# Channels dealt to partitions by threes, one set of convolution diagonals, and row casts on VectorE instead of casting DMAs

## The chip, the cores and the metric

One core of one Trainium2 chip. The metric is the device time of one execution in microseconds (us); the profile's span, from its first to its last instruction, is 1.6 to 2.0 us shorter than that in the runs quoted here. A ratio is the mean time of one kernel's fast runs over the mean of the fast runs of the kernel before in the same rounds, so it is not quite the ratio of the medians that stand beside it.

## The reference

A causal convolution over 7 tokens, with one softmax-normalised set of taps per head (8 heads of 24 channels), then a two-matrix network with the activation h / (1 + exp(-beta h)):

```python
w = softmax(weight, axis=-1)                       # weight: (8, 7)
out = einsum('hk,bskhg->bshg', w, x_unf)           # x: (8, 4096, 192), x_unf: 7 shifted tokens, zeros in front
x = out.reshape(32768, 192)
h = x @ w_in                                       # (192, 2048)
g = h * (1 / (1 + exp(-beta * h)))
y = g @ w_out                                      # (2048, 192), float32
```

## The kernel before

Tokens are worked on in 32 chunks of 1024 (512 from each half of the batch). The 192 channels are cut into three groups of 64; the two batch halves fill the 128 partitions. The matmuls are bf16.

Rows are brought in by casting DMAs on the POOL queue to a buffer in DRAM, then by one large transposing DMA:

```python
def cast(ch):                        # two casting DMAs per chunk, DRAM to DRAM
    ...
    for h in range(2):
        nc.gpsimd.dma_start(out=xd[r0:, :, h, :],
            in_=x_v[p, t0:t1, h, :].rearrange("t (c d) -> t c d", c=NG))
def xpose(ch):                       # one transposing DMA per chunk
    nc.sync.dma_start_transpose(new_xt(ch)[:, :, r0:], xd[r0:].rearrange("t c h d -> t (c h d)"))
```

From the third chunk on the convolution is done on VectorE. A partition's channel differs from group to group, so its taps do too, and a step covers one group (512 columns):

```python
scalar = cw[:, j, k : k + 1]
nc.vector.scalar_tensor_tensor(out=dst, in0=src, scalar=scalar, in1=dst, op0=ALU.mult, op1=ALU.add)
```

The first chunk's convolution runs on TensorE, as seven matmuls with a diagonal matrix for each group. Its start-up matters here:

```python
load_x(x0, 0)                        # SP queue: rows of the first chunk, 2 x 384 KB
load_x(x1, TOK)                      # rows of the second chunk, 2 x 384 KB
... w_out, 4 x 384 KB
load_w_in(0)                         # POOL queue: casting DMA, first quarter of w_in to 64 partitions
...
copy_w_in(0)                         # VectorE: the same weights to partitions 64 to 127
new_ct(0)
for c in range(NG):
    ...                              # 7 diagonal matmuls into pv
    if c < 2:
        nc.vector.tensor_scalar_mul(cts[0][:, c, :], pv, rn[:, c : c + 1])
    else:
        nc.scalar.mul(cts[0][:, c, :], pv, rn[:, c : c + 1])
    if c == 0:
        for b in range(NB):
            cast_rows(x1b, x1, b)    # VectorE casts the second chunk's rows
```

Each chunk then takes 16 steps of six hidden matmuls, one activation on ScalarE and sixteen output matmuls; an output accumulator is reduced on VectorE when it is full.

## Time and profile before

| | before |
|---|---|
| timed runs | 696.6 to 697.2 us, median 697.0 |
| the profiled run | 698.47 us, span 696.7 us |
| PE / ScalarE / VectorE / POOL busy | 99% / 83% / 76% / 9% |
| one chunk in mid-run | 20.9 us |

From the page of the kernel before: the busy time of each engine, and the chain of work that ended last, by engine and by line.

```profile
PE 688.6 (99%) x11339; PEld 497.9 (71%) x11339; DVE 528.2 (76%) x814; ACT 578.5 (83%) x532; POOL 60.6 (9%) x75
...
PE 98%; DMA 1%; ACT 0%; DVE 0%; issue 0%; ACTq 0%
```

The stage table of one chunk (stretch, its length, then busy us of PE, weight loads, VectorE, ScalarE and POOL with the number of instructions, the granted clock, the DMA share and GB/s):

```profile
58.57:79.50 20.93, 20.93 (x358) 15.24 (x356) 18.87 (x29) 17.84 (x17) 10.04 (x12) 1.00 2.08 167
```

PE is busy for all of the chunk, so VectorE and POOL can only matter where PE waits. These places are at the start. TensorE's timeline of the kernel before there (start, length, engine, line, operation; in brackets the idle time in front and what ended it):

```profile
8.82 0.26 PE L293 MATMUL pa<-ident,beta_q 16*128 16x16 f32 x1 [1.43 <-DMA beta_q<-in_moe_beta_dram]
...
9.05 4.97 PE L279 MATMUL ph<-xt,diag 128*128 128x512 f32 x14
13.86 1.79 PE L279 MATMUL pa<-xt,diag 128*128 128x512 f32 x7
15.58 1.47 PE L411 MATMUL ph<-ct,w_in_s 64*128 64x512 bf16 x12
```

In this execution the convolution (L279) starts at 9.05 us, held by the transpose of beta and its DMA, and the twelve first hidden matmuls (L411) run through from 15.58 us. VectorE at that time:

```profile
12.43 0.75 DVE L323 TENSOR_SCALAR ct<-ph,rn 128x512 bf16<-128x512 f32 x1 [0.46 <-PE ph L279]
13.09 1.15 DVE L230 CAST x1b<-x 128x384 bf16<-128x384 f32 x4
14.16 0.74 DVE L323 TENSOR_SCALAR ct<-ph,rn 128x512 bf16<-128x512 f32 x1
```

The casts of the second chunk's rows (x1b) stand between the two convolved columns that VectorE writes, but their data is there: no idle time in front of them.

VectorE's groups over ten chunks in mid-run (out<-in, shapes, count, busy us, mean ns of one, idle time in front):

```profile
L395 DVE SCALAR_TENSOR_TENSOR ct<-xt,cw,ct 128x512 bf16<-128x512 bf16 x181 | 123.2, 745 | 0.0
...
L393 DVE TENSOR_SCALAR ct<-xt,cw 128x512 bf16<-128x512 bf16 x30 | 9.5, 345 | 0.0
```

The chunk of the stage table is an early one, in which VectorE works ahead (24 of these steps, where a chunk has 21 of its own); in mid-run it is busy for 16.4 us of a chunk (164.45 us in ten).

### The profile page before, as it was taken

How to read it: one execution, taken by the hardware profiler on the slowest of the kernel's cores; microseconds unless marked ns; L12 is line 12 of the kernel's file. 1: busy time of each engine (PE TensorE's matmuls, PEld its weight loads, DVE VectorE, ACT ScalarE, POOL GpSimd, SP SyncE). 2: the span in 40 equal slices, each digit the busy share in tenths (PEclk: the TensorE clock that was granted, in tenths of full speed). 3: DMA queues.
4: the chain of work that ended last, by engine and by line, in shares of the span. 5: the costliest groups of instructions: out<-in, count | busy, mean ns of one | idle time of the engine just before them, and what ended most of it. 6: DMA issues, size and time to landing. Idle time of an engine off the chain costs nothing.

```text
span 696.7 us, 24650 instructions
## 1 busy us (share of the span) xinstructions
PE 688.6 (99%) x11339; PEld 497.9 (71%) x11339; DVE 528.2 (76%) x814; ACT 578.5 (83%) x532; POOL 60.6 (9%) x75
## 2 busy tenths in 40 slices
PE   8999999999999999999999999999999999999997
PEld 5477777777777777777777777777777777777776
DVE  4998888977787777787777787777787777787322
ACT  4888888888888888888888888888888888888883
POOL 3724554100000000000000000000000000000000
PEclk9999999999999999999999999999999999999999
DMA  8999999922211223211232211322221222211111
GB/s 226 102 151 168 172 172 176 159 61 71 59 48 49 70 59 71 59 44 53 70 59 71 60 44 50 72 58 70 60 44 52 70 60 71 59 36 37 47 36 59
DMA packets 183064, 54.95 MB, mean 79 GB/s; under 512 B 146336, under 2 KB 182960, under 8 KB 182960
## 3 DMA queue, kind: packets, MB, share of 16 engines
q0 software_dynamic: 96544, 12.92, 29.0%
q1 hardware_dynamic: 86368, 40.45, 24.8%
q8 instruction: 88, 1.44, 0.9%
q14 instruction: 16, 0.13, 0.1%
q10 hardware_dynamic: 48, 0.01, 0.0%
HBM read 28.98 MB, written 37.29 MB: 95 GB/s over the span
## 4 chain that ended last, share of the span: by engine, by line
PE 98%; DMA 1%; ACT 0%; DVE 0%; issue 0%; ACTq 0%
PE ph L411 47%; PE pa L441 25%; PE pb L441 24%; DMA beta_q<-in_moe_beta_dram 1%; PE ph L279 1%; PE pb L279 0%; PE pa L279 0%; ACT g L419 0%; ACT L159 0%; DVE xt L346 0%; DVE w_out_s L308 0%; PE pb L220 0%; ACTq L138 0%; PE ph L213 0%; PE pb L237 0%
## 5 line engine op out<-in xcount | busy, mean ns | idle before, releaser
L419 ACT ACTIVATE g<-ph,beta 128x1024 bf16<-128x1024 f32 x512 | 570.0, 1114 | 99.1 <-PE ph L411 95.0
L441 PEld LDWEIGHTS <-g 64*128 64x128 bf16 x8192 | 352.3, 94 | 121.2 <-issue 1.7
L411 PE MATMUL ph<-ct,w_in_s 64*128 64x512 bf16 x3072 | 415.1, 376 | 0.6 <-ACT g L419 0.6
L395 DVE SCALAR_TENSOR_TENSOR ct<-xt,cw,ct 128x512 bf16<-128x512 bf16 x552 | 375.9, 745 | 0.0
L441 PE MATMUL pa<-w_out_s,g 64*128 64x192 bf16 x4128 | 234.1, 243 | 0.4 <-ACT g L419 0.4
L441 PE MATMUL pb<-w_out_s,g 64*128 64x192 bf16 x4064 | 224.5, 243 | 0.0
L411 PEld LDWEIGHTS <-w_in_s 64*128 64x128 bf16 x3072 | 141.9, 94 | 62.0 <-issue 0.9
L460 DVE TENSOR_REDUCE osb<-pa 128x384 f32<-128x768 f32 x64 | 61.3, 958 | 121.9 <-PE pa L441 121.5
L460 DVE TENSOR_REDUCE osb<-pb 128x384 f32<-128x768 f32 x63 | 60.0, 953 | 31.2 <-PE pb L441 31.1
L104 POOL DMA_DIRECT2D xd<-in_x_dram x60 | 54.4, 909 | 49.7 <-DMA xd<-in_x_dram 48.4
L393 DVE TENSOR_SCALAR ct<-xt,cw 128x512 bf16<-128x512 bf16 x92 | 30.3, 359 | 0.2 <-DMA xt<-xd 0.2
L213 PE MATMUL ph<-zeros 128*128 128x512 bf16 (+2 forms) x13 | 5.3, 475 | 1.3 <-DVE warm L158 1.3
L325 ACT ACTIVATE ct<-pa,rn 128x512 bf16<-128x512 f32 x1 | 0.7, 687 | 5.8 <-PE pa L279 5.8
L457 ACT COPY osb<-pb 128x192 f32<-128x192 f32 x1 | 0.3, 319 | 5.8 <-PE pb L441 5.8
L279 PE MATMUL ph<-xt,diag 128*128 128x512 f32 x14 | 5.0, 520 | 0.0
L192 DVE COPY w_in_s<-w_in_s 64x1536 bf16<-64x1536 bf16 x4 | 3.0, 760 | 1.8 <-DMA w_in_s<-in_moe_w_in_dram 1.7
L279 PEld LDWEIGHTS ph<-xt,diag 128*128 128x128 f32 x14 | 3.6, 259 | 1.0
L346 DVE COPY xt<-pb 128x768 bf16<-128x768 bf16 x2 | 1.9, 958 | 2.6 <-PE pb L237 2.6
L308 DVE TENSOR_TENSOR w_out_s<-w_out_raw,beta_r 128x768 bf16<-128x768 f32 x4 | 3.8, 948 | 0.0
L279 PE MATMUL pb<-xt,diag 128*128 128x512 f32 x7 | 3.5, 497 | 0.0
L279 PEld LDWEIGHTS pb<-xt,diag 128*128 128x128 f32 x7 | 1.3, 186 | 3.0 <-issue 3.0
L213 PEld LDWEIGHTS <-zeros 128*128 128x128 bf16 x13 | 1.6, 129 | 2.2 <-DVE warm L158 1.3
(58 smaller groups left out, 37.5 us busy)
## 6 DMA issues: line engine op xcount, KB each, us to landing
out_dram<-osb SPq DMA_DIRECT2D x127, 192.0 KB, 2.1
xd<-in_x_dram POOLq DMA_DIRECT2D x54, 198.0 KB, 15.1
x<-in_x_dram SPq DMA_DIRECT2D x4, 384.0 KB, 4.6
w_out_raw<-in_moe_w_out_dram SPq DMA_DIRECT2D x4, 384.0 KB, 9.6
xd<-in_x_dram POOLq DMA_DIRECT2D x6, 192.0 KB, 15.4
w_in_s<-in_moe_w_in_dram POOLq DMA_DIRECT2D x4, 192.0 KB, 8.6
xt<-xd SPq DMA_TRANSPOSE x30, 4.6
out_dram<-osb SPq DMA_DIRECT2D x2, 96.0 KB, 1.8
```

The source lines that it names most:

```text
L104: nc.gpsimd.dma_start(out=xd[r0:, :, h, :], in_=x_v[p, t0:t1, h, :].rearrange("t (c d) -> t c d", c=NG),)
L192: nc.vector.tensor_copy(w_in_s[DG : 2 * DG, :, cols], w_in_s[0:DG, :, cols])
L213: nc.tensor.matmul(pf[:, 0, 0:cols], zeros[:, 0:128], zeros[:, 0:cols], start=True, stop=True)
L279: nc.tensor.matmul(pv, diag[:, c, k, :], xt[:, o : o + TOK], start=(k == 0), stop=(k == K - 1))
L308: nc.vector.tensor_tensor(w_out_s[:, fcs, :], w_out_raw[:, fcs, :], beta_r[:, fcs].unsqueeze(2).to_broadcast((128, NQ, D)), ALU.mult,)
L346: nc.vector.tensor_copy(xt[:, :, t : t + 2 * BLK].rearrange("p c (q b) -> p c q b", b=2), halves[i].rearrange("p c b q -> p c q b"),)
L393: nc.vector.tensor_scalar_mul(dst, src, scalar)
L395: nc.vector.scalar_tensor_tensor(out=dst, in0=src, scalar=scalar, in1=dst, op0=ALU.mult, op1=ALU.add)
L411: nc.tensor.matmul(ph[:, h, :], w_in_s[rows, j, fc * 128 : (fc + 1) * 128], cts[s][rows, j, :], start=(j == 0), stop=(j == NG - 1),)
L419: nc.scalar.activation(gs[s][:, fc], ph, AF.Silu, scale=beta[:, fc : fc + 1])
L441: nc.tensor.matmul(self.po[:, r, b * D : (b + 1) * D], g[rows, fc, self.h, q * BLK : (q + 1) * BLK], w_out_s[rows, fc, :], start=(self.don ...
L460: nc.vector.tensor_reduce(dst, self.po[:, :, 0 : nb * D].rearrange("p r n -> p n r"), axis=mybir.AxisListType.X, op=ALU.add,)
```

## The change

Channel 3p + c goes to partition p of group c. All three groups of a partition then belong to one head and share its taps: one set of seven diagonals in place of three, one spread matmul in place of three, and one VectorE step of 1536 columns in place of three of 512. Rows come in as fp32 by ordinary DMAs, VectorE casts them and deals out the channels, and four small DMAs per chunk transpose them from SBUF. Less prominent, the first quarter of w_in is now loaded as fp32, twice, ahead of the second chunk's rows, and cast on ScalarE; and the transpose of beta moves behind 14 convolution matmuls.

```diff
+    def load(ch): ...                # two fp32 DMAs per chunk, SP queue
+    def cast(ch, h):
+        nc.vector.tensor_copy(xbs[ch][:, :, :, h, :],
+            xfs[ch][:, h].rearrange("q b (p c) -> q b c p", c=NG))
     def xpose(ch):
-        nc.sync.dma_start_transpose(new_xt(ch)[:, :, r0:], xd[r0:]...)
+        for b in range(NB):
+            nc.sync.dma_start_transpose(xt[:, :, HALO + b * BLK : HALO + (b + 1) * BLK],
+                xbs[ch][:, b].rearrange("q c h p -> q (c h p)"))
 ...
     load_x(x0, 0)
+    for r in range(2):
+        nc.sync.dma_start(out=w_in_raw[r * DG : (r + 1) * DG], in_=w_in_v[:, :, 0:FW])
     load_x(x1, TOK)
 ...
-    load_w_in(0)
 ...
-    pb = pc[:, 1, 0:NF]
-    nc.tensor.transpose(pb, beta_q, ident[0:NF, 0:NF])
 ...
+    nc.scalar.copy(w_in_s[:, :, 0:FW], w_in_raw)
 ...
-    copy_w_in(0)
 ...
+        if c == 1:
+            pb = in_b()[:, 0, 0:NF]
+            nc.tensor.transpose(pb, beta_q, ident[0:NF, 0:NF])
+            nc.vector.tensor_copy(beta, pb)
+            nc.vector.reciprocal(beta_r, beta)
 ...
-            src = xts[s][:, j, o : o + TOK]
-            scalar = cw[:, j, k : k + 1]
+            src = xts[s][:, c0:, o : o + TOK]
+            scalar = cw[:, k : k + 1]
```

(The tap loop, the halo copies and the places where loads, casts and steps are queued change with it.)

## The prediction

> **What bounds the kernel now.** TensorE. The page gives PE 99% busy of a 696.7 us span, VectorE 76%, ScalarE 83%; the chain that ended last is 98% PE. In the stage table a chunk of 1024 tokens takes 20.92 us (37.65 to 58.57, 58.57 to 79.50), 1.307 us for each of 16 steps: six 512-column hidden matmuls in three pairs and eight pairs of 192-column output matmuls. These stream 3072 columns, 2.35 per ns: almost no gap is left. 32 chunks are 669 us. The other 28 are the start (first hidden matmul at 15.58 us), extra work and stalls in the first chunk, and the end.
>
> **The repeated part.** No repeated PE or ScalarE work changes. On VectorE, per chunk, 18 multiply-add steps of 512 columns (start to start 0.67 us in the timeline) and 3 first steps (0.27) become 6 steps of 1536 columns (my estimate 1.74 us: 1600 ns at one column per 0.96 GHz cycle, plus the 0.14 left over in 0.67) and one first step (0.54): 12.9 us becomes 11.0. Added are two row casts of 768 columns with source step 3 (estimate 0.55 to 1.0 us each, from the 384-column cast's 0.31) and the halo copy (0.16). With four reductions at 0.88 that is 16 to 17 us of 20.92, as before (16.4). VectorE stays off the critical path: a finished accumulator waits for at most 3 us of queued VectorE work, and its bank is needed again about 5 us later. POOL loses its 60 casting DMAs; nothing on the chain waits for them. The four small transposes per chunk are issued about 15 us before their first reader; one large one took about 5 us. I expect 20.9 us per chunk again.
>
> **What reaches the critical path: the start.**
> - The beta transpose waited for its DMA (6.05 us on the chain) and held the first convolution matmul until 9.05 us; it moves behind 14 of these. They then wait for the last copy of transposed rows (ends 7.83) and one set of diagonals; strided row casts may add 0.3 us each. First convolution matmul at 8.0 to 8.6 us: 0.5 to 1.1 gained.
> - Part of it is lost: these matmuls follow each other every 0.42 us until about 11.5 us, then every 0.22. The Trainium skill, "TensorE: Matmul & The Clock Gate", section "What's actually happening", states that the array runs at half clock until one busy window of about 3.4 us, and that the window is free-running; the two spacings agree. If the switch stays at its time, an earlier start runs more matmuls slowly.
> - The later weight spread takes 0.83 us of PE for six matmuls; two remain: about 0.5 us saved where PE stalls.
> - The end is unchanged.
>
> **Predicted:** 695.8 us (before 697.1), 80% range 694.0 to 697.6. Faster by over 2%: 1%; within 2%: 96%; slower by over 2%: 3%.
>
> **What would show each step.** Stage table: 20.9 us per chunk. Groups: 1536-column step near 1.8 us, cast under 1.1. VectorE share 70 to 78%, POOL under 2%. Timeline: first convolution matmul at 8.0 to 8.6 us, first hidden one at 14.5 to 15.2 (before 15.58). Waits: no mid-run PE wait on VectorE or DMA.
>
> **What would make it wrong.** Row casts or 1536-column steps so slow that VectorE passes 20.9 us per chunk; transposes so slow to issue on the SP queue that convolution starts late or output stores queue; VectorE blocked in the first chunk on the third chunk's transposes (its first step is queued before the first reduction); the first weights, now loaded as fp32 ahead of the second rows, arriving late.

## More of the kernel before

All runs used here are of state fast.

The profiled run is over 1 us slower than every timed run beside it.

## The result, and the profile after

The changed kernel took 698.05 us (median of 4 fast runs, 697.18 to 698.35) against 696.98 us; ratio 1.0014, 95% interval 0.9996 to 1.0031. It is the same within 2%, as forecast, but outside the stated range of 694.0 to 697.6. In three later controls, on chips 9, 0 and 9 again, it gave 1.0044, 1.0050 and 1.0020: there it is slower by 0.2 to 0.5%, clear of the intervals, and less steady than the kernel before.

| | before | after |
|---|---|---|
| median | 696.98 us | 698.05 us |
| span of the profile | 696.7 us (a late start) | 696.2 us |
| VectorE / POOL busy | 76% / 9% | 75% / 1% |
| one chunk in mid-run | 20.9 us | 20.9 us |

The two spans alone would say that the change won 0.5 us. They mislead, since the first profile fell on an execution that was late at its start (run b_again below).

From the page of the changed kernel, the engines and the chain:

```profile
PE 687.9 (99%) x11332; PEld 521.2 (75%) x11332; DVE 524.8 (75%) x472; ACT 577.9 (83%) x526; POOL 3.5 (1%) x13
...
PE 95%; DMA 2%; DVE 1%; SPq 1%; ACT 0%; issue 0%; DVEq 0%
```

The stage table of one chunk, and VectorE's groups over ten chunks in mid-run:

```profile
58.60:79.50 20.90, 20.90 (x357) 16.02 (x354) 16.45 (x15) 17.81 (x17) 0.00 (x0) 1.00 0.35 96
```

```profile
L395 DVE SCALAR_TENSOR_TENSOR ct<-xt,cw,ct 128x1536 bf16<-128x1536 bf16 x61 | 110.8, 1816 | 1.1
...
L106 DVE CAST xb<-xf 128x768 bf16<-128x768 f32 x20 | 13.6, 679 | 0.0
L393 DVE TENSOR_SCALAR ct<-xt,cw 128x1536 bf16<-128x1536 bf16 x10 | 10.0, 1003 | 0.0
```

The repeated part did what was forecast: the same 20.9 us, VectorE 16.45 us of it, PE without a gap. On VectorE the longer steps save 12.4 us in ten chunks (123.2 to 110.8) and the casts take 13.6, so its load stays as it was (164.51 us in ten chunks, 164.45 before). The start of TensorE's timeline did not do what was forecast:

```profile
7.29 4.56 PE L285 MATMUL ph<-xt,diag 128*128 128x512 f32 x14 [0.28 <-ACT xt L296]
...
11.94 1.87 PE L285 MATMUL pa<-xt,diag 128*128 128x512 f32 x7
13.74 0.39 PE L411 MATMUL ph<-ct,w_in_s 64*128 64x512 bf16 x2
15.76 1.26 PE L411 MATMUL ph<-ct,w_in_s 64*128 64x512 bf16 x10 [1.63 <-DVE ct L327]
```

The convolution starts at 7.29 instead of 9.05 us, and two hidden matmuls run at 13.74. The other ten wait 1.63 us for a column on VectorE and run at 15.76, where all twelve had run at 15.58 before: the whole lead is gone. VectorE shows why:

```profile
10.24 0.75 DVE L327 TENSOR_SCALAR ct<-ph,rn 128x512 bf16<-128x512 f32 x1 [3.02 <-PE ph L285]
12.58 0.74 DVE L243 CAST x1b<-x 128x384 bf16<-128x384 f32 x2 [1.59 <-DMA x<-in_x_dram]
14.32 0.73 DVE L243 CAST x1b<-x 128x384 bf16<-128x384 f32 x2 [0.99 <-DMA x<-in_x_dram]
14.97 0.74 DVE L327 TENSOR_SCALAR ct<-ph,rn 128x512 bf16<-128x512 f32 x1
```

The casts of the second chunk's rows are queued ahead of the second convolved column, and now VectorE stands idle in front of them for their DMA (1.59 and 0.99 us), while the column behind them waits its turn until 14.97 us. The part of the chain from 3.8 to 16 us, in order of time (start, length, what):

```profile
3.82 10.47 DMA x<-in_x_dram
14.29 0.02 issue
14.32 0.73 DVE x1b L243 x2
15.05 0.67 DVE ct L327
15.72 0.04 issue
15.76 1.26 PE ph L411 x10
```

The last rows took 10.5 us from issue to landing; in the kernel before the slowest of the four row loads took 6.6. Two loads of 384 KB now go ahead of them. The stage table of the changed kernel, in stretches of 1 us, shows 196 to 313 GB/s moving between 6 and 11 us; at 250 GB/s those 768 KB are about 3 us (an estimate from these numbers).

### The profile page after: what moved, and what is told of

It is laid out like the page before. It is cut to its first block, busy times and chain, and to the rows that moved or that the text cites. A ratio compares the mean times of both kernels' runs of the same rounds, so it can differ in the third digit from the quotient of the medians.

```text
span 696.2 us, 24403 instructions
## 1 busy us (share of the span) xinstructions
PE 687.9 (99%) x11332; PEld 521.2 (75%) x11332; DVE 524.8 (75%) x472; ACT 577.9 (83%) x526; POOL 3.5 (1%) x13
## 4 chain that ended last, share of the span: by engine, by line
PE 95%; DMA 2%; DVE 1%; SPq 1%; ACT 0%; issue 0%; DVEq 0%
PE ph L411 47%; PE pa L441 24%; PE pb L441 24%; DMA x<-in_x_dram 2%; SPq L127 1%; PE pb L285 0%; DMA xt<-xb 0%; DVE xt L355 0%; SPq L160 0%; SPq L169 0%; ACT g L419 0%; DVE ct L393 0%; DVE osb L460 0%; DVE w_out_s L313 0%; DVE ct L381 0%
## 5 line engine op out<-in xcount | busy, mean ns | idle before, releaser
L441 PEld LDWEIGHTS <-g 64*128 64x128 bf16 x8192 | 368.8, 94 | 104.9 <-issue 1.9
L411 PE MATMUL ph<-ct,w_in_s 64*128 64x512 bf16 x3072 | 423.7, 376 | 2.2 <-DVE ct L327 1.6
L395 DVE SCALAR_TENSOR_TENSOR ct<-xt,cw,ct 128x1536 bf16<-128x1536 bf16 (+1 forms) x186 | 334.6, 1799 | 3.3
L441 PE MATMUL pa<-w_out_s,g 64*128 64x192 bf16 x4128 | 240.4, 243 | 0.4 <-ACT g L419 0.4
L441 PE MATMUL pb<-w_out_s,g 64*128 64x192 bf16 x4064 | 230.2, 243 | 0.0
L411 PEld LDWEIGHTS <-w_in_s 64*128 64x128 bf16 x3072 | 158.6, 94 | 55.5 <-issue 2.8
L106 DVE CAST xb<-xf 128x768 bf16<-128x768 f32 x60 | 40.8, 679 | 0.0
L393 DVE TENSOR_SCALAR ct<-xt,cw 128x1536 bf16<-128x1536 bf16 (+1 forms) x31 | 30.6, 986 | 2.0 <-DMA xt<-xb 2.0
L307 ACT CAST w_in_s<-w_in_raw 128x1536 bf16<-128x1536 f32 x1 | 1.5, 1472 | 4.1 <-DMA w_in_raw<-in_moe_w_in_dram 4.1
L121 DVE COPY xt<-xt 128x18 bf16<-128x18 bf16 x27 | 4.6, 171 | 0.0
```

Source lines behind the costliest of these rows:

```text
L106: nc.vector.tensor_copy(xbs[ch][:, :, :, h, :], xfs[ch][:, h].rearrange("q b (p c) -> q b c p", c=NG),)
L121: nc.vector.tensor_copy(dst, last[:, :, HALO + TOK - PAD :])
L393: nc.vector.tensor_scalar_mul(dst, src, scalar)
L411: nc.tensor.matmul(ph[:, h, :], w_in_s[rows, j, fc * 128 : (fc + 1) * 128], cts[s][rows, j, :], start=(j == 0), stop=(j == NG - 1),)
L441: nc.tensor.matmul(self.po[:, r, b * D : (b + 1) * D], g[rows, fc, self.h, q * BLK : (q + 1) * BLK], w_out_s[rows, fc, :], start=(self.don ...
```

## The experiments

Each call ran its kernels on one chip together with the kernel before. The table gives medians in us, of the kernel and of the kernel before on that chip.

| run | chip | this | before | ratio | 95% |
|---|---|---|---|---|---|
| b_again | 9 | 697.05 | 697.12 | 0.9998 | 0.9986 to 1.0010 |
| a_again | 9 | 700.82 | 697.12 | 1.0044 | 1.0030 to 1.0059 |
| a_ct1first | 9 | 697.88 | 697.12 | 1.0022 | 1.0010 to 1.0034 |
| a_x1first | 9 | 697.13 | 697.12 | 0.9994 | 0.9980 to 1.0007 |
| a_oldw | 10 | 696.25 | 697.24 | 0.9984 | 0.9971 to 0.9998 |
| a_oldw_late | 10 | 696.13 | 697.24 | 0.9984 | 0.9971 to 0.9997 |
| b_latebeta | 10 | 697.86 | 697.24 | 1.0007 | 0.9992 to 1.0021 |
| a_oldw_cast2 | 10 | 696.16 | 697.24 | 0.9984 | 0.9968 to 1.0000 |
| a_again2 | 0 | 700.36 | 696.92 | 1.0050 | 1.0037 to 1.0064 |
| a_warm | 0 | 699.83 | 696.92 | 1.0039 | 1.0027 to 1.0051 |
| b_neww | 0 | 697.87 | 696.92 | 1.0012 | 0.9998 to 1.0026 |
| a_best | 0 | 695.59 | 696.92 | 0.9978 | 0.9966 to 0.9991 |
| a_again3 | 9 | 698.14 | 697.04 | 1.0020 | 1.0008 to 1.0033 |
| a_holdlate | 9 | 698.19 | 697.04 | 1.0019 | 1.0005 to 1.0032 |

### b_again: the kernel before, unchanged

> The kernel before, unchanged, as a control. Its profiled execution took 698.47 us while its timed ones took 696.6 to 697.2, so its profile may show a start that is about 1.4 us worse than usual. Theory A (that profile was an outlier of the start): ratio 1.000 with an interval under 0.2% wide, and in this profile the first hidden matmul group is complete, or the chunk stage begins, about 1 us earlier than the 37.65 us of the first profile. Rival (the profiler adds 1.4 us to this kernel alone): the profiled time is again near 698.4 and the stage begins at 37.6.

Its time was that of the kernel before, and its profiled run was an ordinary one (697.29 us, span 695.6). Its TensorE timeline:

```profile
7.31 0.28 PE L293 MATMUL pa<-ident,beta_q 16*128 16x16 f32 x1
...
7.87 5.02 PE L279 MATMUL ph<-xt,diag 128*128 128x512 f32 x14
12.73 1.79 PE L279 MATMUL pa<-xt,diag 128*128 128x512 f32 x7
14.45 1.47 PE L411 MATMUL ph<-ct,w_in_s 64*128 64x512 bf16 x12
```

Beta landed 4.7 us after its issue, not 6.1, and its transpose ran without waiting. The convolution starts at 7.87 us and the hidden matmuls at 14.45. So theory A holds: my profile showed an execution that was 1.1 us late at its start (and 1.1 us longer in its span, 696.7 against 695.6). Such executions occur: of the 42 runs of the kernel before three took over 698.4 us (and one 2568 us, which is not counted as fast). In this ordinary one beta did not gate the convolution, and the mark that the changed kernel had to beat was near this run's 14.45, not 15.58.

### a_again: the changed kernel, unchanged, as a control

> The changed kernel, unchanged, on the same chip as the next two. If the first result holds: ratio 1.001 to 1.002 (about 698 us); the second convolved column waits for rows of the second chunk and the ten hidden matmuls of the first pair start near 15.8 us; the first reduction waits for the third chunk's transposes (about 2 us of VectorE). If the first result was noise of the chip: ratio 0.998 to 1.000.

It was slower than both alternatives allowed: 1.0044. Its rows landed still later, and after the wait came something new. TensorE's timeline, and its stage table (the clock is the third number from the end):

```profile
14.33 0.39 PE L411 MATMUL ph<-ct,w_in_s 64*128 64x512 bf16 x2 [0.49 <-ACT w_in_s L307]
17.94 2.32 PE L411 MATMUL ph<-ct,w_in_s 64*128 64x512 bf16 x10 [3.22 <-DVE ct L327]
20.19 0.82 PE L250 MATMUL pb<-ident_b,x1b 128*128 128x128 bf16 x6
21.04 1.47 PE L411 MATMUL ph<-ct,w_in_s 64*128 64x512 bf16 x6
22.43 0.77 PE L250 MATMUL pb<-ident_b,x1b 128*128 128x128 bf16 x6
```

```profile
14.00:16.00 2.00, 0.39 (x2) 0.11 (x3) 0.68 (x2) 0.87 (x2) 0.00 (x0) 1.00 1.16 248
16.00:18.00 2.00, 0.06 (x2) 0.06 (x3) 1.48 (x4) 0.00 (x0) 0.00 (x0) 0.55 1.15 246
18.00:20.00 2.00, 2.00 (x10) 0.60 (x9) 0.25 (x1) 0.13 (x1) 0.00 (x0) 0.50 1.12 305
20.00:22.00 2.00, 1.98 (x14) 0.96 (x12) 0.95 (x2) 1.99 (x2) 0.00 (x0) 0.50 1.07 314
```

TensorE idles for 3.22 us, the granted clock falls to a half, and the next four groups take 2.32, 0.82, 1.47 and 0.77 us where ordinary ones take 1.26, 0.51, 0.82 and 0.51: 2.28 us more by that sum. The Trainium skill, "TensorE: Matmul & The Clock Gate", section "What's actually happening", says that the array falls back to half clock after an idle window of about 3.4 us and that the windows run freely. The fall itself agrees, its length does not: a wait of 1.63 us in the first profile left the clock at 1.00, but waits of 3.22 us here, 2.61 us in a_again2 and 2.13 us in a_x1first, all shorter than that window, did not. Nor does the whole sum reach the end: idle gaps between these groups shrink, and from the third hidden matmul to the later weight spread it is 6.31 us here (17.94 to 24.25) against 4.56 in the first profile (15.76 to 20.32), 1.75 us more. A late load was thus paid for twice here.

### a_ct1first: the second column ahead of the casts

```diff
-        if c == 0:
-            for b in range(NB):
-                cast_rows(x1b, x1, b)
         if c == 1:
             ...
             nc.vector.reciprocal(beta_r, beta)
+            for b in range(NB):
+                cast_rows(x1b, x1, b)
```

> Changed kernel with the casts of the second chunk's rows queued on VectorE after the second convolved column and beta, instead of before them; the DMAs are the same. Theory 1 (in-order VectorE stands waiting for the late second rows and with it the column that TensorE waits for): TensorE does not idle at 14 to 15.8 us, hidden matmuls run through from 13.7 us, the first swish activation starts near 14.9 instead of 16.84, and the time falls by 0.5 to 1.7 us against the changed kernel (ratio to before 0.998 to 1.000); the gain is cut where VectorE later waits for transposes. Rival 2 (the loss is in the repeated part or in the first chunk's later stage): same time as the changed kernel within 0.3 us.

The median fell by 2.9 us against a_again, but it hides two groups (697.8 three times, 699.7 and 699.95); by the ratios the gain is 0.22%, about 1.5 us, as expected, though the two intervals just overlap and 1.0022 is above the 0.998 to 1.000 that I had expected against the kernel before. TensorE's line:

```profile
15.54 1.47 PE L410 MATMUL ph<-ct,w_in_s 64*128 64x512 bf16 x12
```

The twelve hidden matmuls ran through, as theory 1 has it, but from 15.54 us and not 13.7: in this profile the first chunk's own rows were late as well, the convolution started at 8.39, and its first 14 matmuls took 5.25 us, not 4.56. So the wait behind the casts is real, and it is not all.

### a_x1first: the second rows loaded ahead of the weights

```diff
-    for r in range(2): ...w_in_raw...
     load_x(x1, TOK)
+    for r in range(2): ...w_in_raw...
```

> Changed kernel with the second chunk's rows loaded ahead of the fp32 first weights. Theory 1a (it is only the order of the loads that counts, the queue delivers in order at a fixed rate): second rows land near 9 us, the weights near 12.5 to 14.3, their cast on ScalarE ends near 15.8, so the first hidden matmul starts near 15.5 to 16 and the time is that of the changed kernel within 0.5 us. Rival 1b (the weights' loads into 64 partitions each are slow by themselves and hold up what is behind them): weights land soon after the rows, near 12.5, cast done by 14, and the time falls by about 1 us.

Neither theory had the time right. 1a's landings were met: the rows landed at 9.32 us and were cast from 9.92 without waiting, the weights landed at 13.33 and were cast on ScalarE from 13.41. But that is only 0.6 us later than in the control on that chip (12.80), so a queue of fixed rate in strict order is too simple. The hidden matmuls started after a wait for the weights, and the clock was at 0.50 between 16 and 18 us:

```profile
14.93 2.46 PE L411 MATMUL ph<-ct,w_in_s 64*128 64x512 bf16 x12 [2.13 <-ACT w_in_s L307]
```

The median was 3.7 us under the control and equal to the kernel before.

### a_oldw: the old load path of the first weights put back

```diff
-    for r in range(2):
-        nc.sync.dma_start(out=w_in_raw[r * DG : (r + 1) * DG], in_=w_in_v[:, :, 0:FW])
+    load_w_in(0)
 ...
-    nc.scalar.copy(w_in_s[:, :, 0:FW], w_in_raw)
+    copy_w_in(0)
```

> Changed kernel with the load of the first quarter of the input weights put back as before: a casting DMA of 64 rows on the POOL queue and a VectorE copy, in place of two fp32 loads in the same queue ahead of the second rows and a ScalarE cast. Theory 1a (these fp32 bytes ahead of the second rows are what ate the gain): second rows land by 9 us as before, no idle of TensorE between the convolution and the hidden matmuls, no stretch at half clock, first convolution near 7.4, hidden ones run through from about 14.0; ratio 0.9985 to 0.9995, i.e. 0.3 to 1 us under the kernel before and 2 to 3 us under the changed one as measured on the same chip. Rival (the rest of the change costs too): ratio 1.001 or more.

Theory 1a holds against its rival: ratio 0.9984, just below the 0.9985 to 0.9995 expected. Two of its numbers were not met or not tested: the second rows landed at 10.82 us, not by 9 (early enough for casts that start at 11.96), and the changed kernel itself was not run on this chip. TensorE and VectorE in this run:

```profile
7.47 4.34 PE L282 MATMUL ph<-xt,diag 128*128 128x512 f32 x14 [0.27 <-ACT xt L293]
...
11.90 1.88 PE L282 MATMUL pa<-xt,diag 128*128 128x512 f32 x7
13.71 1.60 PE L408 MATMUL ph<-ct,w_in_s 64*128 64x512 bf16 x12
```

```profile
11.96 1.38 DVE L240 CAST x1b<-x 128x384 bf16<-128x384 f32 x4
13.26 0.74 DVE L324 TENSOR_SCALAR ct<-ph,rn 128x512 bf16<-128x512 f32 x1
```

The casts do not wait, and all twelve hidden matmuls run through from 13.71 us, 0.74 us ahead of an ordinary run of the kernel before. With this one part undone the change is a gain of 0.16%, and 696.25 us lies inside the range that I had predicted for the whole. This is the main result: the repeated part costs nothing, and the load path of the first weights is what turned a small gain into a small loss (the changed kernel's ratios are from other calls, so this compares across chips; a_x1first shows the order of the loads on one chip).

Where the time lies, worked out from the starts of the hidden matmuls in three traces (us; the parts add up to the span):

| | b_again | changed (first profile) | a_oldw |
|---|---|---|---|
| start to the 13th hidden matmul | 16.91 | 18.01 | 16.30 |
| on to the last one of the first chunk | 17.51 | 17.35 | 17.35 |
| the second chunk | 20.83 | 21.08 | 20.83 |
| each of the other 30 chunks | 20.92 | 20.92 | 20.92 |
| last hidden matmul to the end | 12.73 | 12.13 | 11.97 |
| span | 695.6 | 696.2 | 694.0 |

So a_oldw wins 0.6 us at the start in these traces, and 0.76 us at the end, which I had overlooked. From the end of VectorE's last operation to the end of the span it is 3.37 us in b_again, 2.78 in the changed kernel and 2.61 in a_oldw, and SyncE has 11, 8 and 9 semaphore instructions there. In the last row all four traces of the kernel before and its variants have 12.57 to 12.75 us, all twelve of the changed kernel and its variants 11.97 to 12.15. Which part of the change shortens it is not tested. The first row is the one that moves from trace to trace (run b_latebeta below): of the 0.99 us between the two medians, the other rows take 0.92, which leaves about 0.1 us for the start (an estimate from these numbers). The small gain is mostly the end's.

### a_oldw_late: no early step in front of the first reduction

```diff
-            pops = u % 2 if s > 0 else u in (4, 6, 8, 9, 11, 12, 13, 15)
+            pops = u % 2 if s > 0 else u in (4, 6, 8, 9, 11, 12, 13)
```

> The same with the first convolution step of the third chunk not queued in the first chunk's last slot, so that the first reduction does not stand behind a step that waits for the transposes. Theory: the 2 us wait of VectorE for transposes goes from before the first reduction, TensorE no longer waits for it near 40 us, 0.2 to 0.6 us less than a_oldw. Rival: that wait was hidden, equal within 0.15 us.

The wait went (VectorE's first reduction started at 35.50 instead of 36.88 us), the time did not move: the rival holds. The start was not the same in the two profiles: here the hidden matmuls did not run through, since the second column came late again, with VectorE held not by the rows but by the weights' DMA (its copy of them starts at 10.45 us):

```profile
13.93 1.26 PE L408 MATMUL ph<-ct,w_in_s 64*128 64x512 bf16 x10 [0.76 <-DVE ct L324]
```

In a_oldw the accumulator was needed again at 38.11 us and was free before. In the profile of the changed kernel the same wait ended at 40.00 us, and TensorE used the accumulator at 40.05, 0.64 us after the group in front of it had started; 0.41 is usual (39.61 to 40.02 in the kernel before), so there it cost about 0.23 us (that chunk is 0.25 us longer, 21.08 us).

### b_latebeta: only the beta transpose moved, in the kernel before

```diff
-    pb = pc[:, 1, 0:NF]
-    nc.tensor.transpose(pb, beta_q, ident[0:NF, 0:NF])
-    fill(1)
+    fill(1, 256)
 ...
+        if c == 1:
+            pb = in_b()[:, 0, 0:NF]
+            nc.tensor.transpose(pb, beta_q, ident[0:NF, 0:NF])
+            nc.vector.tensor_copy(beta, pb)
+            nc.vector.reciprocal(beta_r, beta)
```

> Kernel before with only the beta transpose moved behind 14 convolution matmuls, one part of the change. My prediction's reading (beta's DMA gates the convolution): 0.5 to 1.1 us faster, ratio 0.9985 to 0.9993. What the second profile of the kernel before suggests (beta landed at 7.3 us and the row copies on ScalarE gate, the first profile was an outlier): first convolution matmul near 7.8, ratio 0.9995 to 1.0005.

1.0007, within its interval no change, and the convolution started at 7.87 us as in b_again. The gain of 0.5 to 1.1 us that I had put on this move is not there. TensorE's timeline shows something else that I had missed:

```profile
7.87 5.73 PE L279 MATMUL ph<-xt,diag 128*128 128x512 f32 x14 [0.27 <-ACT xt L290]
...
15.51 1.47 PE L412 MATMUL ph<-ct,w_in_s 64*128 64x512 bf16 x12
```

From the same start the hidden matmuls come 1.06 us later than in b_again (14.45), 0.71 us of that because the 14 convolution matmuls took 5.73 us, not 5.02: their spacing of 0.43 us gave way to 0.23 later. In the four traces of the changed kernel, which is the same program each time, these 14 take 4.35, 4.56, 4.59 and 5.73 us; in all sixteen traces they take 3.48 to 5.73. So a start read from a single trace carries over 1 us that comes from no edit; the medians decide.

### a_oldw_cast2: twice the row casts

```diff
-        nc.vector.tensor_copy(xbs[ch]...)
+        for _ in range(2 if ch > 3 else 1):
+            nc.vector.tensor_copy(xbs[ch]...)
```

> a_oldw_late with each row cast from the fifth chunk on done twice (same values): about 1.2 us more VectorE work in each of 28 chunks, 34 us in all. If VectorE is off the critical path in the repeated part: same time as a_oldw_late within 0.3 us, chunk still 20.92 us. If it is on it: up to 34 us slower.

The same time as a_oldw_late (696.16 and 696.13). One chunk in a_oldw_late, then in this run:

```profile
58.57:79.50 20.93, 20.93 (x356) 15.24 (x354) 18.20 (x16) 17.83 (x16) 0.00 (x0) 1.00 0.35 96
```

```profile
58.57:79.50 20.93, 20.93 (x356) 15.24 (x354) 19.49 (x18) 17.82 (x17) 0.00 (x0) 1.00 0.35 96
```

VectorE does 1.29 us more and the chunk is as long as before. VectorE is off the critical path of the repeated part, so the 1536-column steps, which save it 1.2 us of fused steps per chunk, had nothing to win there.

### a_again2 and a_warm: does the half clock cost by itself?

```diff
+    for _ in range(10):
+        nc.tensor.matmul(pv2[:, 1, :], zeros[:, 0:128], zeros, start=True, stop=True)
```

> Changed kernel unchanged, control for the next three on the same chip. Ratio between 1.001 and 1.005, by how late the second rows land on this chip; the ten held hidden matmuls start between 15.7 and 18 us.

> Changed kernel with ten 512-column matmuls of zeros (about 2.2 us) put into the stretch in which TensorE waits for the second convolved column; nothing else changes. Theory 3 (where that wait is long, the granted clock falls to a half for some us afterwards, and this costs beside the wait): no clock below 0.9 in this run's table after 12 us, and where the control waits until 17.5 us or later the time falls by 1 to 2 us; where it waits until 16 only, no change or up to 0.3 us more. Rival (the clock's fall costs nothing, or the zeros don't hold it): same time as the control within 0.3 us in long waits too.

The control gave 1.0050. In its profile the ten hidden matmuls started at 16.90 us and took 2.32 us; the table shows a clock of 0.65 and 0.50 from 16 to 20 us. With the zeros the clock stayed at 1.00, the first twelve hidden matmuls took 1.47 us, and the ratio was 1.0039. So the clock's fall can be held off; what that is worth is not clear of noise, as the intervals overlap and the gain is 0.5 us by the medians, not 1 to 2 (the control waited until 16.90 us, between the two cases that I had named): the zeros themselves waited 0.78 us for ScalarE to read their accumulator and ended at about 18.4 us, after the column that TensorE waited for was ready (VectorE finished it at 17.9). The size of the clock's share is thus read from the trace of a_again (1.75 us there) and not confirmed.

### b_neww: only the new load path, in the kernel before

```diff
     load_x(x0, 0)
+    for r in range(2): ...w_in_raw...
     load_x(x1, TOK)
-    load_w_in(0)
 ...
-    copy_w_in(0)
+    nc.scalar.copy(w_in_s[:, :, 0:FW], w_in_raw)
```

> Kernel before with only the load of the first quarter of the input weights done the new way: two fp32 loads ahead of the second rows, a ScalarE cast. Theory 1a (this one part makes the loss): second rows land between 12.5 and 16.5 us instead of 8.5, the second convolved column and the hidden matmuls wait for them, ratio 1.001 to 1.006. Rival (it hurts only with the rest of the change): ratio 0.999 to 1.0005.

1.0012, interval 0.9998 to 1.0026: the low end of what theory 1a said, and not clear of zero. The last rows were cast at 13.74 us, and the second column was begun at 14.28 and ready at 15.03, a little late for hidden matmuls that started at 14.57: the twelve took 1.77 us where b_again has 1.47. In this kernel, whose convolution ends later, the load path alone thus hurt little.

### a_again3 and a_holdlate: why the rows are later in the changed kernel

In the changed kernel the casting DMAs of the other three quarters of w_in start at 5.2 us, in b_neww at 7.3. They are held back by a value that is now ready earlier. This run holds them on a later one.

```diff
-    nc.gpsimd.tensor_copy(hold, eu[0:1, 0:1])
+    nc.gpsimd.tensor_copy(hold, rn[0:1, 0:1])    # and the three loads behind it
```

> Changed kernel unchanged, control for the next run on the same chip. Ratio to before 1.001 to 1.006; casting DMAs of the other weights start at 5.2 us; last rows of the second chunk are cast between 14.3 and 16.5 us.

> Changed kernel with the casting DMAs of the other three quarters of the input weights held until about 7.3 us (on the reciprocal instead of the spread weights). Theory 4 (their earlier start, a by-product of the shorter spread, shares the DMA engines with the second rows and delays them): last rows cast 1 to 2 us earlier than in the control, at 12.5 to 14 us, the wait of TensorE under 1.5 us, no half clock, ratio 0.999 to 1.002, i.e. 1 to 3 us under the control. Rival (these DMAs do not matter to the rows, the chip's or run's spread explains it): rows as late as in the control, times equal within 0.5 us.

The theory fell. The DMAs started at 7.45 us, the last rows were cast at 14.88 (control 15.62), and the times were equal (1.0019 and 1.0020). Why the rows land at 14.3 to 16.5 us in the changed kernel and near 13.7 in b_neww stays open; b_neww is a single profile of a quantity that moves by 1 to 2 us from run to run.

### a_best: a version that beats both

a_oldw_late with the first weights' casting DMA issued first on POOL, the copy to the upper partitions on ScalarE, and the second rows' casts behind the second column:

```diff
+    load_w_in(0)
     sel = setup.tile([H, 2, DG], FP32)
 ...
-    copy_w_in(0)
+    nc.scalar.copy(w_in_s[DG : 2 * DG, :, 0:FW], w_in_s[0:DG, :, 0:FW])
 ...                                  # and the casts moved as in a_ct1first
```

> a_oldw_late with the first weights' casting DMA issued first on POOL, their copy to the upper rows on ScalarE, and the second rows' casts queued after the second convolved column. Theory (after the old load path is back, the start hangs on the first weights and on VectorE standing for them): the hidden matmuls run through from the end of the convolution, 12.8 to 13.9 us depending on when the clock comes up, 0.2 to 1 us under a_oldw_late's 0.9984, i.e. 0.997 to 0.998. Rival: the row loads get slower by the earlier DMA and the convolution starts later, no gain.

0.9978, 1.3 us under the kernel before by the medians, correct. The weights' copy on ScalarE, ahead of the last convolved column and the first activations:

```profile
8.11 1.47 ACT L315 COPY w_in_s<-w_in_s 64x1536 bf16<-64x1536 bf16 x1 [0.83 <-DMA w_in_s<-in_moe_w_in_dram]
14.29 0.69 ACT L325 ACTIVATE ct<-pa,rn 128x512 bf16<-128x512 f32 x1 [4.71 <-PE pa L281]
```

The weights are in place at 9.6 us, and neither they nor the rows hold the hidden matmuls any longer; these followed the convolution without a wait, at 14.19 us in this profile (later than the 12.8 to 13.9 expected: the 14 convolution matmuls took 4.95 us). The interval overlaps a_oldw_late's, measured on another chip, so the gain of this last step over a_oldw_late is not settled.

## Why the prediction was wrong

- **Repeated part: right.** 20.9 us per chunk, PE without a gap. The 1536-column step took 1.82 us (estimate 1.74), the cast 0.68 (0.55 to 1.0), VectorE 75% and POOL 1%. The first step took 1.00 us where I said 0.54; it did not matter, as a_oldw_cast2 shows for more than that. The four small transposes were in time.
- **"First convolution matmul at 8.0 to 8.6 us: 0.5 to 1.1 gained": failed.** It started at 7.29 us, but in the three other traces of the kernel before and its variants it starts at 7.87 or 7.88, not 9.05. I took one late execution for the rule, though its own time of 698.47 us stood beside timed runs of at most 697.19. b_latebeta shows no gain from moving beta (1.0007, 0.9992 to 1.0021).
- **The missing term: the load queue.** In "What reaches the critical path: the start" no time is set against the 768 KB of fp32 weights ahead of the second rows. I had named "the first weights, now loaded as fp32 ahead of the second rows, arriving late" as a risk, and looked at the weights; in the first profile their cast ran from 11.31 to 12.78 us, in time (in a_again it ended at 14.27 and held the first two hidden matmuls for 0.49 us). It was the rows behind them that came late, and through VectorE's order the column that TensorE needed: "first hidden one at 14.5 to 15.2" became two matmuls at 13.74 and ten at 15.76. a_oldw puts the whole load path of these weights back, queue, cast and copy, and lands at 696.25 us, 0.16% under the kernel before. That this lies in my range is in part luck: 0.76 us of it comes from the end, where I had forecast nothing. a_x1first changes only the order of the loads and recovers 3.7 us of its control's median; a_ct1first moves only the casts and recovers about 1.5 us, not quite clear of noise.
- **"An earlier start runs more matmuls slowly": not borne out.** From the first convolution matmul to the first hidden one it is 6.45 us in the changed kernel's first profile, 6.53 and 6.58 in the two of the kernel before. The two spacings are there, but the point where they change moves from run to run (see b_latebeta). What cost time was another thing, the clock falling again after a long wait, 1.75 us in a_again.
- **The later weight spread: right in its size.** 0.83 us became 0.38, but by the end of the first chunk only 0.16 us of that was left (17.51 to 17.35 in the table).
- **"The end is unchanged": failed, in the change's favour.** It is 0.60 us shorter (12.73 to 12.13); why is not tested.
- **The first reduction behind the transposes: a named risk that came true in the first profile and cost about 0.23 us there.**

Shown by runs: the load path's part, the order of the loads above all, VectorE off the path in mid-run, no gain from beta's move. Seen in the traces, with a run that points the same way but is not clear of noise: the wait behind the casts. Argued from traces only: that the half clock's share is up to 1.75 us where the clock falls. Open: why the rows land later in the changed kernel than in b_neww, and why the end is shorter.

## What to carry to other kernels

When the engine that bounds the kernel has no gap in the repeated part, a change elsewhere can only move the start and the end, so cost both as carefully as the loop: every byte put into a queue ahead of something, and everything that an engine has queued in front of what the bound engine waits for. Before reading a start from a profile, compare the profiled run's own time with the timed runs; where it differs by more than what you hope to gain, take a second profile. Split the spans of both profiles into the same stages: that shows at once where they differ. Put a load that is needed later behind what is needed sooner, and queue work on late data behind work that others wait for.

## What the Trainium skill lacked or had wrong

- "Vector Engine (DVE) Microarchitecture Reference", section 5.1, and "VectorE: DVE Perf Modes", section "What auto-detection actually checks", let a one-source bf16 operation run four elements per cycle if the outermost counts are even, or odd and equal on both sides. The first step took 0.345 us for 512 columns in mid-run and 0.48 us for 1024 in two blocks, but 1.00 us for 1536 in three blocks: 0.135 us more for the second 512 and 0.52 us more for the third. This looks like a breach and is none: the trace records its source as three blocks of 512 and its destination as one run of 1536, so the outermost counts are 3 and 1536. What neither section says is that adjoining blocks of a destination, three in the program, can reach the instruction as one run.
- Section 5.1 of the first also lets an fp32 to bf16 copy use both ports whatever the source's step; this agrees: the cast of 768 columns at a step of three took 0.68 us, less than the 0.80 us of one column at a time at the pace of the fused steps (1071 ns for the 1024 columns between 745 ns at 512 and 1816 at 1536). No page gives the cost of a step of three in such a copy: two casts of 384 columns took 0.63 us at unit step and 0.74 us at a step of three.
- "TensorE: Matmul & The Clock Gate" gives about 3.4 us of idleness for the fall to half clock. In these runs shorter waits were followed by it: 3.22 us (a_again), 2.61 us (a_again2, clock 0.50 from 17 to 20 us) and 2.13 us (a_x1first, 0.50 from 16 to 18 us); one of 1.63 us was not. A table of idle lengths and outcomes would help more than the one figure.
- No page says how late a load lands behind others in one queue while other queues run: the last 384 KB of rows took 6.5 to 6.6 us from issue to landing in the kernel before, and 9.8 (b_neww) to 12.6 us (a_again) behind 768 KB more.
